# Another written order of all engines and queues, and a tile of its own for the products of dots and softmax weights, in a one-core kernel with a hand-written issue order

## The chip, the cores and the metric

The kernel runs on one core of one Trainium2 chip. The metric is the device time of one execution in microseconds; a time is the median of several runs. Five engines work side by side, each through its own list of instructions in the order in which the program wrote them: TensorE (PE, with its weight loads PEld), VectorE (DVE), ScalarE (ACT), GpSimd (POOL, which here issues the gathers and the accumulating stores) and SyncE (SP, which issues all other transfers). Transfers run on 16 DMA engines. An engine waits at the head of its list when an input is not there; what stands behind waits with it.

## What is computed

An input `x` of 2048 rows by 448 columns is normalised, and three things are added: `x` itself, a state-space convolution (S4) and a layer of 4096 tiny experts (PEER, 16 heads, one expert for each head and row).

```python
    def _A_ref(u, A_re, A_im, B_re, B_im, C_re, C_im, log_dt, Dskip):
        ...
        P = jnp.exp(logdA[:, :, None] * l[None, None, :])
        K = jnp.einsum("dn,dnl,dn->dl", Cc, P, dB).real
        ...
        y = (lambda x, *d: x.transpose(*d))(y, 0, 2, 1) + u * Dskip[None, None, :]
        return y

    def _B_ref(x, w_q, k1, k2, u, v):
        ...
        s1 = jnp.einsum("nhd,ed->nhe", q1, k1)
        s2 = jnp.einsum("nhd,ed->nhe", q2, k2)
        i1 = jnp.argsort(-s1, axis=-1)[..., :K]
        i2 = jnp.argsort(-s2, axis=-1)[..., :K]
        ...
        g = _softmax(top_s, axis=-1)
        ue = u[top_e]
        ve = v[top_e]
        act = _gelu(jnp.einsum("nd,nhkd->nhk", xf, ue))
        out = jnp.einsum("nhk,nhk,nhkd->nd", g, act, ve)
        return out.reshape(B, S, D)

    x = A_u
    xn = _layernorm(x, axis=-1)
    return x + _A_ref(xn, A_A_re, ...) + _B_ref(xn, B_w_q, B_k1, B_k2, B_u, B_v)
```

The elided part of `_A_ref` convolves every column with its kernel `K` by FFT.

## The kernel before

The work is cut into some 3,400 small steps. A step belongs to one engine, and steps of one kind form a stream (`e_d`, `s4_v`, ...), in which they keep their sequence. `plan()` makes the streams; `Plan.run` then walks a constant string, `ORDER`. Each character names a stream, and the next step of that stream is written. So `ORDER` alone fixes the sequence on every engine and every queue. Buffers come from rings: a step takes a slot and a later step gives it back. The largest ring has 22 slots of 128 x 1024 floats; gathered rows (`ue`), layer-norm tiles, combined weights, products of the convolution and transfers to and from DRAM all share it, and a new tile gets the slot that has been free longest. Waits between engines follow from which tiles a step reads and writes, not from the list of dependencies in the plan, which only forbids orders.

The streams that the text speaks of, with their lines:

- Scores: the weights are combined with the keys on PE (`w_p`, L862), a layer-norm tile is transposed (`sc_t`, L943), scores are made on PE (`sc_p`, L961 and L970), and DVE and ACT find the best key (L985 to L1048). The indices go to DRAM and come back (`ix_st`, `ix_ld`).
- Experts, 16 tiles of rows with 4 groups each, 64 groups: four gathers on POOL (`e_g`, L1083) bring 896 floats for each row, the expert's u and v side by side. DVE makes the dot product of each (`e_d`, L1091). Then, on 128 x 4 numbers, a tanh form of gelu: ACT squares the dots (L1098), DVE makes the cubic (`e_v1`, L1101), DVE multiplies the dots by the softmax weights (`e_v1`, L1110), ACT takes the tanh (L1104), DVE joins the two (`e_v2`, L1107) and spreads the result over a mask (`e_v2`, L1114), and PE uses that as weights to add up the v halves (`e_p`, L1121). After the last group of a tile, ACT copies the sum out (`o_a`, L1132) and POOL adds it to the output in DRAM (`o_st`, L1135).
- S4, 56 batches of 8 columns: exponentials and angles, sines on ACT (L629 to L635), four products on DVE (`s4_v`, L660 to L666), a product on PE (`s4_k1`, L682), a copy on ACT (`s4_k2`, L690), a small addition on DVE (`s4_k2b`, L693), PE again (`s4_k3`, L702), a copy on ACT (`s4_k4`, L706).
- Convolution, in four chunks of columns; the last chunk has 64 of them: PE (`cu1`, `cv1`; L762, L779 for the last chunk), DVE products (`cv3`, L808, in the last chunk L786), PE (`cv5`, L830, last L825), ACT (`cv6`, L837), a store to `t_d` (`cv7`, L842). Then the tiles are loaded back (L1165), multiplied on PE (L1177), and added to the output: for three chunks over ACT and POOL (`f_p`, `f_a` L1184, `f_st` L1191), for the last chunk on DVE (`g_v`, L1181), which reads the output back first (`g_b`, L1155) and stores it (`g_st`, L1189).

The order is written in time: the string starts with loads and layer norm, mixes scores, S4 and experts through the middle, and ends with the last chunk.

Of the kernel before, what the change touches and what calls it, by code (L numbers as in the profile page):

```python
# [172 lines left out]
ORDER = (
    "41H444446H4447H244024HHHH424HH6H4H2H7H12H4HHHHHII7H42H1HNCC42H7282O42D2E842HH8748HH121CDH4CD2KHF4HEE1D14E224HFL4H4CKL7DC"
    "I472K24F72EC4I4F3MD7777E7Y3C5QFJLKL9D56DCEFEP47F48D47C9F9EM8KQLQ48D9FwK97774E7FC4L8K44DCJA947E449YC87C9JFDD47E46H7RF4798"
    "AL8QRCEARF7ADCZDEDRFEFEFKQRHwQLNORHGQ9RHQQPH9SaRRMRTQZHTRQYQNATRRHTRHHJOATSTQQTTTTBRTeHReTTGQTUVQGHbYVMHHWRRQQHHXHxxcHee"
    "RRRPdfSNgxgOyfeHgHHwgQwQIHHIyxPfQKyHgygzggxRQJ!gRT!gHhRYTQLTGRzHgQhTKh#xgHRLxTfRMRNOPeSQygyJxXgx#TQ$yTxgeHQHTfQTyTThxTzR"
    "!HgRg!bHxTfgxRgzTQRe#Q#yyyUycgdz$NybxxRO!Qch!ezRyVQHhH#Rdebyi#STTVIIgxRRHThhYwj$gwyzh!QxK!wgyHQzWTLHRwRQKxLRQHRxy#TN#kR$"
    "HxPMhShghyxyxHOHizxaygHQXH!TyxTjTeK!QThJLTyy%kbXeRzhHRQ&RQKRiJzxP#jHf!Qg#$!eyHHLYRQzhggHkfRghieHHRxxgxSf#jK#ykTyI$lLKTgg"
    "LMeTyZlzmTKm!x!LlKyxzmLlN#xUHM#Tyx$IOgggTxgQTYQwKPhHHQyHfHQyTRwgzLwg!R!gQxhgRhRKgzMhyHTe#HfJHgHw#gLmQxHeehxx$yRyhiNRReeO"  # L180
    "yxjkfgzQQ!gVHVhSP!xg%yTyHzJxTyTHx#QRT#gHxTTyQglRHzThchQ$gH!hTIMdKgg!YQR&TIxRRLWmyYKLiNJhjhzfyR#OgUJk#R$ihaQHjexPyVyHxHeH"
    "zKSkMxgegy!x!hHQfTLHRKzyTexLgMR#g#eVQhfH$HbRgQgwQwglhyWxwZTxXygghyHwHzlRggRmHmH!Yg!TRzyTxiQf#xjke#RHy$HSNOHHIyhxTxlTz!TT"
    "TXXK!yTghQLTzQ#yeTPegxhKhgJhx%#fgmeyxgyIQxyezyLifg$Hjg!cQbRkRhKTg!YgLRzxlKh#UQHg#MgVgx$dQygaRLxHiNyhHxHmzOfPQeygw!R!xjhy"
    "ggzkefgyRRSgxyQ&##RHwQRThhzRVw!HHH$fxTQl!zH##QRehHQgRgiyRHHxgeWRSxewNMHjHxO$HhkTIyhgQgZKLyTxQhlJyTxmyTgKLRigmTQzhx!T!zIx"
    "#xygyMfJ%xgJXTQyPeRRTRg#hx$TgTjfzekQKgy!TRgx!Lxfyhz#y#lTegQRxKUgc$LmeNRSVxVeayOhWhzywQ!hTQiQyRjxgy!hQzygwhRPhXzgxgMT#Rxk"
    "g#ih$R!xdg!xgQQexfwzxy#ZwTRjRhTgkRT#yyNOx$hQxSeTx%ylegfx&zey!gQTyTxgfPT!RTzyyTTexQQgTlgz!#T!#z#myR$yhQQ#UyRVgyRxRxxywz!N"
    "OgiRRy$xP!jSzmhyQhX#yklwn#hgxTxQ$RmTRgwwgVQgixxhhnxhgeefz!yyyy!ggWfxzehjkTxQQx##gTgeXfzyRgl$TQyRRxm!eg!yRzR&%#xhx-Sn#xyz"
    "y!yyn$ioTpT!gzhTaoy#gbqzxojo!h#pqxpcqnyTghgxT!onypzyoTwdgTTp#k$ghigqT#refexhyeXxhqwz!hgxyehsgof!&zUxpoxsepwjXg$wgqpykf#q"
    "nogpghhxoyVbxq#gypqiggg$hnxrg%izxoxyhyjxgyg!kf!Vqyzx&ez##sgghp$ex!xqsooxyfp!zxpjyZ#ge#yk$eetgoqhfggWhqhrggxsynozyhghygoh"
    "sxlxwm!xtwpy!lticgywxpqmdaz#wzi!jgk!l#qghexpXqXhzbejkf#hy$#xhhyghegxmlfhyxe$gylyxge%mxzf!hgmrslg!yzm#igjk#gxnghhlgm$hyix"  # L190
    "gs&jyxyzZkhygghf!xlmg!z#exyyhijz#exhge!fkeggyy!tyfgeggzlghgc(gy$hhw#(ihxjwxdmhg)#zka!*gxhg$x!hifezjkelg#xwglm+f#xege$xxh"
    "wxgfgxy%yhgyyegy)gzi*yg!jh!ghkyzhmlxgfg(xh#gmxZ#g$iyx(hej)hhykhg*feezegigyjxy!fk!+zegg+#alxgmyg#lzy!!wbgzhyh#yfmg)xgxg$h"
    "*hexgyhghigfze#gjgxfgywhk$wx!hlix!+gyZemeecgx-xXwz#gghjyydzgklm#!yhfgghy!e$zgoo#%poggheq#yyohppfegqix$ohpzgyxq!yx!pqhxfg"
    "yyz#xnjeox&xpgrqzgqs#cyo!!oephiqgpoagkqzh$#dfwxgsngogphgrp#gxgyhyfqyqoxZx$ygjewhhgystipkhzfxeox!oq!zghjgohee#swpqrwkeyig"
    "g#hhygpsgojbxtyqhypxsxzp!ogyk!fgz$lhmhqxitpgxqeqhjy#&begkzeegrhles!fxsml#gxm%xytxhlmxy&nl!zm#giyfxjyZkggg#zgygwah!h$glh("
    "mhfgx!ygheeghygz#igj$hexfkyhe(lgzegf#gwgxmg!!x$)gwgyiyygzhxhcxg*xd##hwjykz!n+$glmh!ixhfg(ezgyeyh)%j#xkxeeghfg#yxg(f*gyh)"
    "eyygg$c*zlghimgZh!jggdxkyh!zla)bgmyhfghx#*i+ggfh#gxgeh&x$ehxxzj+yfekgyge!ie!xyggzjgkyghxgzfhx#hlh!mg#gwl$whmei+hh!ggfxxg"
    "ezhgfwyjgwey-gex#yg#xeiyzgxyg!kal$yj!zx%yxhyxghmkz#hc!#hg$ydglxeghfyymggixfgheyegfe!jzh#k#xezg!ylg!Zxgzxhggyy#iggh$yhz#$"
    "wwg!jhkmlymxfwoheyxexh!giphgwqego&oypfxepqqyz#ohx#yxggoz!ppfqg!yjy$gxzeoyr#gqxxozphngigqkoxpgs#%aq!yxo!z$yhpg#ghqejsfpno"
    "gehyrggphs&hyxe#tzfgq$kegofgnxygi!qg!jhexzphxouxqpo#gvnk#ghyqywwpxgwhg$qsihgojyfyezg!kx!pzqopehetgrghhsshoyny#whfuglxlx#"  # L200
    "qmpgymiefvjhgzx$egxgykulx!gmlg!x%yqytxnihymzglgghxhxghr&shhhzixjs#j#k!lvh$mmy!kizxt##jlkyl(ymum$vooqoqyzqy!x!rs)yq,qsqry"
    "(*zsosrsq#xy(zsq)!+!r)*sts+t#t$t*(z#.#+$%.)/:&.-//.::/*;+;;:;")


class Kernel:
# [861 lines left out]
    def experts(s, t):  # L1067
        p = s.p
# [8 lines left out]
        for g in range(4):  # L1077
            Q = {}
            u = (4 * t + g) / 64
            for c in range(4):  # L1080
                def ga(c=c, g=g, Q=Q):
                    ue = Q["ue", c] = s.flat("q", "ue", 2 * D)
                    s.nc.gpsimd.indirect_dma_start(  # L1083
                        out=ue, out_offset=None, in_=s.io["uv"],
                        in_offset=bass.IndirectOffsetOnAxis(ap=s.IDX[t][:, c, g:g + 1].bitcast(U32), axis=0))

                def do(c=c, Q=Q):
                    if c == 0:
                        for k in ("dot", "x2", "th"):
# [1 line left out]
                    s.nc.vector.scalar_tensor_tensor(Q["ue", c][:, :D], Q["ue", c][:, :D], 1.0, B["xr", c], op0=ALU.mult, op1=ALU.mult,  # L1091
                                                     accum_out=Q["dot"][:, c:c + 1])
# [4 lines left out]
            def a1(Q=Q):
                s.nc.scalar.activation(Q["x2"], Q["dot"], AF.Square)  # L1098

            def v1(Q=Q):  # L1100
                s.nc.vector.scalar_tensor_tensor(Q["x2"], Q["x2"], 1 / 0.044715, Q["dot"], op0=ALU.add, op1=ALU.mult)  # L1101

            def a2(Q=Q):
                s.nc.scalar.activation(Q["th"], Q["x2"], AF.Tanh, scale=math.sqrt(2 / math.pi) * 0.044715)  # L1104

            def v2(Q=Q):
                s.nc.vector.scalar_tensor_tensor(Q["th"], Q["th"], 1.0, Q["dot"], op0=ALU.add, op1=ALU.mult)  # L1107

            def v2b(g=g, Q=Q):
                s.nc.vector.tensor_tensor(out=Q["dot"], in0=Q["dot"], in1=s.IDX[t][:, :, 4 + g].bitcast(F32), op=ALU.mult)  # L1110

            def v2c(Q=Q):
                Q["A"] = s.sm.tile([128, 4, 32], F32, name="A", bufs=2)
                s.nc.vector.tensor_tensor(out=Q["A"], in0=s.mask[:, None, :].to_broadcast([128, 4, 32]),  # L1114
                                          in1=Q["th"][:, :, None].to_broadcast([128, 4, 32]), op=ALU.mult)

            def m2(g=g, Q=Q):
                if g == 0:
                    B["po"] = s.pst([128, 512], "po", "po")
                for c in range(4):  # L1120
                    s.nc.tensor.matmul(B["po"][32 * c:32 * c + 32, :D], Q["A"][:, c], Q["ue", c][:, D:],  # L1121
                                       start=(g == 0), stop=(g == 3))
# [138 lines left out]
```

## Time and profile before

| what | value |
|---|---|
| median of 3 runs | 810.61 us (805.64 to 812.17) |
| the profiled execution | 807.42 us, of which its span is 805.7 us |
| busy share of the span | PE 82%, DVE 85%, ACT 66%, POOL 44% |
| mean granted TensorE clock | 0.906 |

A row of the profile's groups gives the source line, the engine, the operation and its tiles, how often it ran, its busy time and the mean of one in nanoseconds, then the time that the engine stood idle just before it and what ended most of that. A row of the waits gives who waited for whom, the total, the number of times and the longest. A row of the timeline gives the start and the duration, and in brackets the idle time before. A row of the stretches gives, for each engine, busy time and number of instructions, then the granted clock, the busy share of the DMA engines and what they moved.

### The profile page before, as it was taken

What the parts mean: (1) busy time and instruction counts of PE and PEld (TensorE: products, weight loads), DVE (VectorE), ACT (ScalarE), POOL (GpSimd) and SP (SyncE); (2) the same over time, 40 slices, a digit from 0 to 9 for tenths busy, and PEclk for the clock granted to TensorE, in tenths of its full rate; (3) what the DMA queues carried; (4) which work ended last, traced back from release to release, by engine and by line L of the source; (5) the groups of instructions that cost most, each with busy time, mean ns of one, the idle gap of its engine ahead of it and who ended that gap; (6) DMA issues with size and microseconds to landing.
All of it is one profiled execution on the core that took longest, in us unless ns stands there. A gap on an engine that the chain in (4) does not pass through costs nothing.

```text
span 805.7 us, 19880 instructions
## 1 busy us (share of the span) xinstructions
PE 664.6 (82%) x7628; PEld 361.1 (45%) x7628; DVE 686.9 (85%) x1727; ACT 533.3 (66%) x1069; POOL 351.6 (44%) x303
## 2 busy tenths in 40 slices
...
PEclk9999999999999999999999995678997665699896
...
GB/s 313 348 335 263 259 224 175 232 204 249 275 199 242 202 202 255 180 252 270 366 300 312 304 286 286 292 291 276 206 286 344 319 222 269 252 264 287 271 253 175
DMA packets 139975, 212.36 MB, mean 264 GB/s; under 512 B 45096, under 2 KB 121896, under 8 KB 139816
## 3 DMA queue, kind: packets, MB, share of 16 engines
q0 software_dynamic: 29120, 124.27, 49.9%
q1 hardware_dynamic: 110760, 86.81, 35.5%
...
## 4 chain that ended last, share of the span: by engine, by line
DVE 33%; PE 24%; ACT 15%; DMA 15%; issue 9%; POOL 2%; SPq 1%; POOLq 0%; DVEq 0%; ACTq 0%
PE sc L961 8%; DVE ue L1091 7%; DMA ue<-in_uv_dram,ig 6%; DVE ph L614 4%; PE wc L862 3%; DVE mg L666 3%; PE po L1121 3%; DVE zi L662 2%; DVE cp L808 2%; ACT CS L635 2%; DVE mx L985 2%; ACT CS L629 2%; ACT CS L632 2%; PE sc L970 2%; PE up L724 2%
## 5 line engine op out<-in xcount | busy, mean ns | idle before, releaser
L1083 POOL DMA_INDIRECT ue<-in_uv_dram,ig x256 | 308.2, 1204 | 364.2 <-PE po L1121 101.4
L961 PE MATMUL sc<-W,xt 128*128 128x512 f32 x384 | 181.2, 611 | 8.6 <-ACT xt L946 7.8
L1091 DVE SCALAR_TENSOR_TENSOR ue<-ue,xr 128x448 f32<-128x448 f32 x256 | 155.7, 619 | 26.0 <-DMA ue<-in_uv_dram,ig 24.1
L961 PEld LDWEIGHTS sc<-W,xt 128*128 128x128 f32 x384 | 69.3, 191 | 100.8 <-issue 86.2
L1121 PE MATMUL po<-ue,A 128*32 128x448 f32 x512 | 74.0, 654 | 23.4 <-DVE A L1114 9.2
L682 PE MATMUL kp<-mg 128*32 128x64 f32 x1792 | 65.8, 244 | 22.2 <-DVE mg L666 7.9
L590 ACT ACTIVATE mg<-lg 128x512 f32<-128x512 f32 x112 | 63.1, 603 | 17.2 <-PE lg L579 16.7
L682 PEld LDWEIGHTS kp<-mg 128*32 128x32 f32 x1792 | 48.1, 124 | 49.4 <-issue 13.2
L662 DVE TENSOR_TENSOR zi<-mg,CS 128x1024 f32<-128x1024 f32 x56 | 68.3, 1219 | 0.0
L666 DVE TENSOR_TENSOR mg<-mg,CS 128x1024 f32<-128x1024 f32 x56 | 68.3, 1219 | 0.0
L682 PE MATMUL kp<-zi 128*32 128x64 f32 x1792 | 65.7, 242 | 0.0
L614 DVE CUSTOM_DVE_ANT_0 ph<-st,ph 128x512 uint16<-128x512 uint16 (+2 forms) x84 | 65.2, 776 | 0.5
L635 ACT ACTIVATE CS<-CS,halfpi 128x1024 f32<-128x1024 f32 x56 | 64.4, 1150 | 0.8
L629 ACT ACTIVATE CS<-ph 128x1024 f32<-128x1024 int32 x56 | 62.0, 1107 | 3.9 <-DVE ph L614 3.1
L632 ACT ACTIVATE CS<-ph 128x1024 f32<-128x1024 int32 x56 | 62.6, 1117 | 0.0
L702 PE MATMUL vp<-f,kt 128*64 128x128 f32 x448 | 41.3, 317 | 19.5 <-DVE kt L693 11.3
L985 DVE TENSOR_REDUCE mx<-sc 128x8 f32<-128x512 f32 x64 | 43.7, 683 | 14.5 <-PE sc L970 9.6
L682 PEld LDWEIGHTS kp<-zi 128*32 128x32 f32 x1792 | 50.3, 126 | 0.2
L579 PE MATMUL lg<-lc,rt 32*128 32x512 f32 x112 | 38.8, 544 | 12.0 <-ACT mg L590 7.9
L830 PE MATMUL ip<-cp,e 64*128 64x256 f32 x384 | 44.7, 382 | 2.9 <-DVE cp L808 2.8
L702 PEld LDWEIGHTS vp<-f,kt 128*64 128x64 f32 x448 | 27.5, 155 | 43.1 <-DVE kt L693 16.7
L798 PE MATMUL U<-VU,g 128*64 128x128 f32 x384 | 41.3, 294 | 6.0 <-ACT us L803 3.4
(244 smaller groups left out, 1219.2 us busy)
## 6 DMA issues: line engine op xcount, KB each, us to landing
...
ue<-in_uv_dram,ig POOLq DMA_INDIRECT x256
...
```

The costliest lines, as they stand in the source:

```text
L614: s.nc.vector.tensor_tensor(out=rw(n, 2 * n), in0=rw(0, n), in1=o["st"][:, k, b0:b0 + 2].rearrange("p b h m x -> p (b h m x)")[:, None].to ...
L629: s.nc.scalar.activation(CS[:, 1].rearrange("p (m r x) -> p m r x", r=16, x=2), four(s.ph), AF.Sin, scale=SC)
L632: s.nc.scalar.activation(B["CS"][:, 0].rearrange("p (m r x) -> p m r x", r=16, x=2), four(s.ph), AF.Abs)
L635: s.nc.scalar.activation(B["CS"][:, 0], B["CS"][:, 0], AF.Sin, scale=-SC, bias=s.halfpi)
L662: V.tensor_tensor(out=zi[:, 512:], in0=mg[:, 512:], in1=CS[:, 1], op=ALU.mult)
L666: V.tensor_tensor(out=mg[:, 512:], in0=mg[:, 512:], in1=CS[:, 0], op=ALU.mult)
L682: s.nc.tensor.matmul(kp[32 * c:32 * c + 32, 64 * gi:64 * gi + 64], T[ri][:, 1024 + m:1056 + m], view(T[ri], m, [[512, 2], [1, 32]]), start ...
L702: s.nc.tensor.matmul(vp[64 * ri:64 * ri + 64, 128 * gi:128 * gi + 128], B["kt"][:, 64 * gi:64 * gi + 64], s.f1[:, ri], start=True, stop=True)
L961: s.nc.tensor.matmul(B["sc", q].rearrange("p a b -> p (a b)"), B["xt"][:, i], w, start=(q % 2 == 0 and i == 0), stop=(q % 2 == 1 and i == 2))
L1083: s.nc.gpsimd.indirect_dma_start(out=ue, out_offset=None, in_=s.io["uv"], in_offset=bass.IndirectOffsetOnAxis(ap=s.IDX[t][:, c, g:g + 1].b ...
L1091: s.nc.vector.scalar_tensor_tensor(Q["ue", c][:, :D], Q["ue", c][:, :D], 1.0, B["xr", c], op0=ALU.mult, op1=ALU.mult, accum_out=Q["dot"][: ...
L1121: s.nc.tensor.matmul(B["po"][32 * c:32 * c + 32, :D], Q["A"][:, c], Q["ue", c][:, D:], start=(g == 0), stop=(g == 3))
```

## The change

`ORDER` is another string of the same length, with the same number of characters for every stream; every engine and the SP queue get another sequence. Of 538 steps on PE 122 keep their place and a step moves by 1.9 places on average; on DVE 87 of 1429 keep it (6.5 places on average, at most 90), on ACT 115 of 863 (3.2), on SP 47 of 285 (3.6). The 256 gathers keep their places among each other, and of the 28 accumulating stores on POOL 25 keep theirs among each other.

In `experts`, the product of the dots and the softmax weights (L1110) goes to a tile `dw` of its own in place of overwriting `dot`, and the plan lets it follow the dots directly; its stream still puts it behind the cubic of the same group. The join (L1107) reads `dw`.

```diff
 ORDER = (
-    "41H444446H4447H244024HHHH424HH6H4H2H7H12H4HHHHHII7H42H1HNCC42H7282O42D2E842HH8748HH121CDH4CD2KHF4HEE1D14E224HFL4H4CKL7DC"
...
-    "qmpgymiefvjhgzx$egxgykulx!gmlg!x%yqytxnihymzglgghxhxghr&shhhzixjs#j#k!lvh$mmy!kizxt##jlkyl(ymum$vooqoqyzqy!x!rs)yq,qsqry"
-    "(*zsosrsq#xy(zsq)!+!r)*sts+t#t$t*(z#.#+$%.)/:&.-//.::/*;+;;:;")
+    "44H444HH1HH2704HH7HH2HHH46HH7HH24444I6H4444H47H8CH22NI2H4241DE4HHC88142OC78D4D127H4H1EKECH74C44FLKF4CHHDL47HDEEFKDFFL24H"
...
+    "%gkuolhgmileqxhpwlgjyxzhtmxiqhg!!gjmggzrxglshshklkhuh#hlmmmhhyytij&x#kxixxyyjvz!$xv(kxllmymo!oqqqryysqszox(rs#y#yy)o$ysz"
+    "y!zz!#!tz!*#q,q()#q#rtss($qr*+)ts$+s*t..+).//%&::-./:/*;;:+;;")
...
-                        for k in ("dot", "x2", "th"):
+                        for k in ("dot", "x2", "th", "dw"):
                             Q[k] = s.sm.tile([128, 4], F32, name=k, bufs=2)
...
             def v2(Q=Q):
-                s.nc.vector.scalar_tensor_tensor(Q["th"], Q["th"], 1.0, Q["dot"], op0=ALU.add, op1=ALU.mult)
+                s.nc.vector.scalar_tensor_tensor(Q["th"], Q["th"], 1.0, Q["dw"], op0=ALU.add, op1=ALU.mult)
 
             def v2b(g=g, Q=Q):
-                s.nc.vector.tensor_tensor(out=Q["dot"], in0=Q["dot"], in1=s.IDX[t][:, :, 4 + g].bitcast(F32), op=ALU.mult)
+                s.nc.vector.tensor_tensor(out=Q["dw"], in0=Q["dot"], in1=s.IDX[t][:, :, 4 + g].bitcast(F32), op=ALU.mult)
...
             y = p.add("e_a", "ACT", 100, a1, deps=[v])
-            y = p.chain("e_v1", "DVE", [(75, v1), (75, v2b)], deps=[y])
+            y = p.add("e_v1", "DVE", 75, v1, deps=[y])
+            yw = p.add("e_v1", "DVE", 75, v2b, deps=[v])
             y = p.add("e_a", "ACT", 100, a2, deps=[y], tset="E|S|A")
-            y = p.chain("e_v2", "DVE", [(75, v2), (dv(128), v2c)], deps=[y, s.C["mask"]], take=("A",), give=("gel",))
+            y = p.chain("e_v2", "DVE", [(75, v2), (dv(128), v2c)], deps=[y, yw, s.C["mask"]], take=("A",), give=("gel",))
```

In the string, `x` is a gather, `y` a dot, `z` an ACT step of the gelu, `!` is `e_v1`, `#` is `e_v2`, `$` is `e_p`; `h` is `s4_v`, `i` `s4_k1`, `j` `s4_k2`, `k` `s4_k2b`, `l` `s4_k3`, `m` `s4_k4`; `u` is `cu1`, `o` `cv1`, `q` `cv3`, `r` `cv5`, `s` `cv6`, `t` `cv7`; `%` is `o_a`, `&` `o_st`; `(`, `)`, `*`, `+` are the load, PE, ACT and POOL steps of the first three chunks' ends, and `-`, `.`, `/`, `:`, `;` those of the last chunk (read back, load, PE, DVE, store).

More of the change, by code (lines that the diff above doesn't have):

```diff
@@ L178 @@
[L178 to L197, printed above, removed]
@@ L198 @@
-    "ezhgfwyjgwey-gex#yg#xeiyzgxyg!kal$yj!zx%yxhyxghmkz#hc!#hg$ydglxeghfyymggixfgheyegfe!jzh#k#xezg!ylg!Zxgzxhggyy#iggh$yhz#$"
-    "wwg!jhkmlymxfwoheyxexh!giphgwqego&oypfxepqqyz#ohx#yxggoz!ppfqg!yjy$gxzeoyr#gqxxozphngigqkoxpgs#%aq!yxo!z$yhpg#ghqejsfpno"
-    "gehyrggphs&hyxe#tzfgq$kegofgnxygi!qg!jhexzphxouxqpo#gvnk#ghyqywwpxgwhg$qsihgojyfyezg!kx!pzqopehetgrghhsshoyny#whfuglxlx#"
-    "qmpgymiefvjhgzx$egxgykulx!gmlg!x%yqytxnihymzglgghxhxghr&shhhzixjs#j#k!lvh$mmy!kizxt##jlkyl(ymum$vooqoqyzqy!x!rs)yq,qsqry"
@@ L202 @@
-    "(*zsosrsq#xy(zsq)!+!r)*sts+t#t$t*(z#.#+$%.)/:&.-//.::/*;+;;:;")
+    "44H444HH1HH2704HH7HH2HHH46HH7HH24444I6H4444H47H8CH22NI2H4241DE4HHC88142OC78D4D127H4H1EKECH74C44FLKF4CHHDL47HDEEFKDFFL24H"
+    "27EC4J42HMF2HDC227KLI272223QEI47DC44E4346CDFFDK441C4QE4C9FDE978L88FDRQ9M4CREE94J74497J75RCKF5F8LQ4KCD977R71D4wE77E9778CL"
+    "FFDEDAE6YFF7AYK9QHHLQANH7OQRHR9GR8S8AH9wQZH9HRaTwRHAQGHeRQYTHRQTHGQTRTRYHNHRHOSTQJTAQGMTHTeTHbQTRTTReTQUcQdQRVeNfRIVOWgg"
+    "PXRQRfQPPPxBRRggHSxQTfgRxTyHeTRggIRZxTgwMXJxQKTyxHLyyfgQKLgzxQRh!!HRNRyyOz#xSPyyHQgzT!MH#QQxxggzgJTT$h!RyhTxRxR#HQRgfhgT"
@@ new lines @@
+    "#HQyTbghyh$yzQx!fHz!#NxyReOyiQ#TeHTHx$gyxRwYHeyxRTwxzQeUKHSeVQR!whgLhHwRjgHgcQQKQx!PRydzgY#yHRLHTbyIJRINHR#ThgThHx$bhHhH"
+    "TOgKcLkRHVaTyMSdxgzxgT!!QiHxQzRyKHxQj#eHTyPTQRTyTHhxQfyTz!Hk#H%LggRRz$JhQMxH!iHjRRfhHRgxKg#TLHkyIfYhygTW#exyeTSexiX$KLYg"
+    "lxKlLNMeyjzO!IHQzHgxKy!mygLPK#yTkTMxmQ#Hyl$ggwJQRHhzLRh!Thgmg!HezQfxhRex#gK#eQHwRwxThheHyxLgRgHR$y%QfggRHNxxOUiyjwfyzQ!z"
+    "TMx!hy#byZSQggVVT#cQeHxyHRykHlgHHgzx$a!hRxJHgQ!gQHzTIYmhKTy&x#gLTh#digXIKTeQRyRTLJYP$fNjggTRhRlxOgeHyyHkHQzfKgh!gLxmzHHh"
@@ new lines @@
+    "T!yexxlHPiH#QmjeRHTK#SJWHhRHhf$yxQgLgURXeggRhQyhHkYgyVgQiz!gQzg!TlMHwTHeHVNMRgHw#HRTIj#xbww&xmxxhOkh$eTyeQPRRhSxyKhTQlfT"
+    "eyyLIgJe%zy!T!QxRXmzQxYT#xKT#T$gLfyHyxKRTgQLgfyhzHHRx!!RhxzMg#QNxg#Hh$ggOyyiTHhxjKTTyHyggzUHR!RkHhPxcR!hZiQQQyRxgazSd#Qf"
+    "jyHxygkRgLH#RlHRgyzhh$iHMw!TeHT!HVQHhRmgfQNHgz#eO#$Rgx%xwIfThyRTjKTWygSQxwxekVLeJTKlQlywyexQxggLPxzIQ!gygR!TTyRRmgzhgxRi"
+    "TT#Q#gyy$QjzhZ!zexx!gkhMTKxefLhgTXKe#Thh#yyTRJh$imReLegfxNggOyRyfxMyhggxyQQz!!xxUgzxRyS#gjWagh#RlQ$QQRkyTThRglQwXzThgmgg"
```

18 lines of the change are left out of this document (15 added, 3 removed).

## The prediction

> **What bounds the kernel now.** I read the page first: the busy shares, the DMA queues and the chain that ended last.
>
> ```profile
> span 805.7 us, 19880 instructions
> PE 664.6 (82%) x7628; PEld 361.1 (45%) x7628; DVE 686.9 (85%) x1727; ACT 533.3 (66%) x1069; POOL 351.6 (44%) x303
> PEclk9999999999999999999999995678997665699896
> q0 software_dynamic: 29120, 124.27, 49.9%
> q1 hardware_dynamic: 110760, 86.81, 35.5%
> DVE 33%; PE 24%; ACT 15%; DMA 15%; issue 9%; POOL 2%; SPq 1%; POOLq 0%; DVEq 0%; ACTq 0%
> ```
>
> Three resources are near their limit together: DVE at 85%, PE at 82%, and the DMA engines at 49.9 + 35.5 = 85.4% of the span. None of them owns the chain (DVE has a third of it). A new sequence of the same work can take only idle time; DVE has 805.7 - 686.9 = 118.8 us of it. The second view, busy time by stage, says where.
>
> ```profile
> 0.00:150.00 150.00, 124.81 (x444) 51.11 (x445) 111.70 (x240) 72.04 (x169) 28.12 (x35) 1.00 0.80 272
> 150.00:400.00 250.00, 230.39 (x1839) 99.16 (x1838) 232.35 (x628) 158.44 (x341) 111.31 (x97) 0.99 0.77 240
> 400.00:750.00 350.00, 272.50 (x4579) 182.87 (x4577) 319.57 (x800) 285.50 (x520) 196.83 (x158) 0.82 0.94 282
> 750.00:806.00 56.00, 36.91 (x768) 27.95 (x768) 23.29 (x63) 17.28 (x40) 15.30 (x15) 0.80 0.94 230
> ```
>
> The columns after the stretch are PE, PEld, DVE, ACT, POOL, the clock and the DMA share. DVE's idle time is 38.3 us up to 150 (PE is the bound there once the weights come in), 17.7 us from 150 to 400 (PE and DVE both at 92 to 93%), 30.4 us from 400 to 750 (DVE 91%, DMA 94%), and 32.7 us in the last 56. The third view is DVE's waits, first from 100 to 760, then from 760 to the end.
>
> ```profile
> DVE ue L1091 <- DMA ue<-in_uv_dram,ig: 24.1, 23, 2.9
> DVE kt L693 <- ACT kt L690: 6.1, 7, 1.8
> DVE th L1107 <- ACT th L1104: 3.3, 7, 1.6
> ...
> DVE bb L1181 <- PE po L1177: 13.5, 4, 11.1
> DVE cp L786 <- PE U L779: 4.3, 2, 2.6
> DVE th L1107 <- ACT th L1104: 3.6, 1, 3.6
> DVE kt L693 <- ACT kt L690: 2.6, 1, 2.6
> ```
>
> In the middle, dots that wait for their gather are the largest item, 24.1 us in 23 waits; in the tail the waits are a chain of steps that cannot overlap. These two places carry the forecast.
>
> **The change part by part.** *The tile `dw`.*
>
> ```profile
> L1110 DVE TENSOR_TENSOR dot<-dot,ig 128x4 f32<-128x4 f32 x64 | 10.2, 160 | 0.4
> 763.03 0.20 ACT L1104 ACTIVATE th<-x 128x4 f32<-128x4 f32 x1
> 763.11 0.16 DVE L1110 TENSOR_TENSOR dot<-dot,ig 128x4 f32<-128x4 f32 x1
> ```
>
> The 64 products keep their 160 ns. Before, too, the tanh did not wait for the product: it starts at 763.03, the product of the same group at 763.11. Only the plan's list tied them, and in the stream the product still follows the cubic, which has waited for the square already. So the tile by itself is worth 0; its cover is that no wait existed. Bounds: 0 to the 0.4 us that DVE idled before L1110. No instruction is added or removed, and the changes of function set on ACT, each a table load, number 61 in both strings.
>
> *The start.*
>
> ```profile
> 18.12 1.33 PE xtp L943 x5
> 103.36 1.58 DMA idx_d<-ix
> ```
>
> PE now begins with the combined weights and not with the transposes that waited for the first layer norm. Only the 1.33 us of transposes can be gained, if the weights are there sooner; but from PE step 38 to 58 the sequence is the same as before, so I take 0. Against it: the index store that starts at 103.36, on which all gathers hang, now has 3.3 us more DVE work written ahead of it (layer-norm steps, two angle steps, two maxima of the next tile). The first dots also stand behind 3.3 us more work, which covers it; price 0, bounds -1.3 to +3.3. On SP the weight loads move ahead of a layer-norm load and an `xr` load; on its own list the last of them is at place 58, before at 62. Covered while PE is busy; without the cover it is within these bounds.
>
> *The middle.* Thousands of moves can't be priced one by one, so I count distances in the two strings, with each step's duration from the trace.
>
> ```profile
> L1083 POOL DMA_INDIRECT ue<-in_uv_dram,ig x256 | 308.2, 1204 | 364.2 <-PE po L1121 101.4 <-issue 47.0 <-DMA ig<-idx_d 46.6
> L1091 DVE SCALAR_TENSOR_TENSOR ue<-ue,xr 128x448 f32<-128x448 f32 x256 | 155.7, 619 | 26.0 <-DMA ue<-in_uv_dram,ig 24.1 <-DMA xr<-xn_d 0.9 <-PE vp L702 0.8
> ```
>
> Gathers wait mostly for a slot that PE must free (101.4 us). Counting takes and gives of the 22-slot ring, 4.3 slots are free on average when a gather is written before, 5.2 after; for gathers 64 to 95 it is 3.0 against 5.6. With 430 takes in some 760 us, 0.9 of a slot means a release 1.6 us earlier. Against it, the DVE work written between a gather and its dot falls from 6.2 to 5.6 us on average. The net, 1.0 us earlier, stands beside a mean wait of 24.1/23 = 1.05 us. Were it uniform, nearly all 24.1 us would go; it is not (the distance to the dot rises for some gathers and falls for others), and from 400 on the DMA engines are 94% busy. I take a quarter, -6, with the ends -24 and +23 (the second is a rival below). For the small addition L693, 21 of 56 have under 1 us of DVE work between ACT's copy and themselves before, 10 after: half of the 6.1 us goes, -3, ends -6 and 0. The sines' products (17 against 16 of 448 under 1 us) and the joins behind the tanh (17 against 14 of 64 under 0.3 us) hardly change: 0. That is -9 of DVE waiting. Where DVE stops waiting, PE or the DMA engines are late next, at 92% and 94% in the stages; I count 0.6 of it, between the chain's third and all: -5.4, say -5.
>
> *The tail.* Here the sequence can be followed step by step.
>
> ```profile
> 752.10 0.63 DVE L1091 SCALAR_TENSOR_TENSOR ue<-ue,xr 128x448 f32<-128x448 f32 x1 [1.77 <-DMA ue<-in_uv_dram,ig]
> 761.43 1.22 DVE L666 TENSOR_TENSOR mg<-mg,CS 128x1024 f32<-128x1024 f32 x1
> 762.64 1.72 PE L1121 MATMUL po<-ue,A 128*32 128x448 f32 x8
> 768.25 0.96 PE L1121 MATMUL po<-ue,A 128*32 128x448 f32 x8
> 769.14 3.02 PE L779 MATMUL U<-VK,g 128*64 128x64 f32 x96
> 770.34 1.29 DVE L786 TENSOR_TENSOR cp<-us,U 128x512 f32<-128x512 f32 x2 [2.65 <-PE U L779]
> 779.37 0.68 DVE L786 TENSOR_TENSOR cp<-us,U 128x512 f32<-128x512 f32 x1
> 780.97 2.00 PE L825 MATMUL ip<-cp,e 64*128 64x256 f32 x16
> 785.31 0.96 PE L1121 MATMUL po<-ue,A 128*32 128x448 f32 x8 [0.45 <-DVE A L1114]
> 787.25 0.86 POOL L1135 DMA_DIRECT2D out_dram<-ob  x1 [1.05 <-ACT ob L1132]
> 787.25 6.86 DMA out_dram<-ob
> 794.91 3.88 DMA tl<-t_d
> ```
>
> Let V be the end of the last S4 product, 762.65 before. (a) In the new order four dots, numbers 244 to 247, stand behind V and not before it: 4 x 0.62 = 2.5 us, and one of them waited 1.77 us for its gather. V comes up to 4.3 us earlier; ACT's sines may stop it sooner, so I take 3.4. (b) Before, PE ran the sum of group 60 (1.72 us) between V and the last batch's product, and that of group 61 (0.96 us) ahead of the last chunk's products, which start at 769.14, V + 6.5. Now the first follows the last batch's product and the second the chunk's first products. The small addition (L693) stands behind the four dots, at about V + 3, and with some 1.5 us through L702 and L706, an estimate, L779 starts at V + 4.5. (c) From there DVE has more to do than before, seven dots and some ten small steps besides the eight products: 8 x 0.68 + 7 x 0.62 + 2 = 11.8 us against the 9.7 from 770.34 to 780.05. It starts 1.2 us after L779, as before, so the last product ends at V + 17.5, as it did (780.05 is V + 17.4). (d) Before, the last expert sum (785.31, V + 22.7) waited for the tanh, 3.6 us late in ACT's list; now the tanh comes first, and the sum follows the last L825 and one L1177 of about 1.1 us, at V + 20.6: 2 us earlier. The accumulating store at 787.25 (6.86 us to land) and the load behind it (3.88 us) close the run and shift with it. Together -5.4. Against it, the last gather now waits for the first L779 group and its dot stands ahead of the last four products; a late one holds the convolution, 0 to 2 us. POOL's list keeps the last stores behind the last gather. I take -4, ends -7 and +2.
>
> [...]
>
> ```profile
> 758.76 0.19 PEld L682 LDWEIGHTS kp<-mg 128*32 128x32 f32 x8 [3.71 <-ACT tq L837]
> 760.00:765.00 5.00, 3.40 (x49) 2.00 (x53) 3.77 (x13) 1.46 (x5) 0.38 (x1) 0.50 0.66 209
> 604.74 1.10 PE kp L682 x64
> 685.92 1.86 PE kp L682 x64
> ```
>
> After the gap of 3.71 us the clock is 0.50, and a batch of L682 takes 1.10 us in one place and 1.86 in another. [...]
>
> *The sum.* -4 - 5 = -9 against the profiled execution's 807.42 gives 798.4. The median, 810.61, stands 3.2 us above that execution, so I forecast 798.4 + 3.1 = 801.5 for a median.
>
> **The rivals.** *No net gain.* With PE, DVE and the DMA engines within 3% of each other, a wait shortened on one shows again on the next; for it speaks the chain without an owner. The middle gives 0 and the tail up to -4: 806.6 to 810.6.
>
> *Slower, through gathers that come too late.* 30 of 256 gathers have under 1.5 us of DVE work between them and their dot, before 22. If the eight each paid the longest wait seen, 2.9 us, that is +23, of which 0.6 counts, +14; less the tail's 4, +10: 810.6 + 10 = 820.6. It decides once the dots wait over 20 us more than their 24.1. The DMA share of 0.94 speaks for it, the older slots against.
>
> [...]
>
> *The change does nothing.* The tile alone does nothing; the order as a whole can't be said to do nothing, so this falls into the first rival.
>
> **How the numbers follow.** A measurement of this kernel tells about 1% from no change, 802.5 to 818.7. The forecast has 0.48, of which 0.37 lies under 802.5 and 0.11 above. No net gain has 0.30 (0.03 faster, 0.22 within, 0.05 slower, since the unpriced moves go both ways). Late gathers have 0.15 (0.02 within, 0.13 slower). The clock has 0.07 (0.05 and, with wider gaps, 0.02 slower). Together faster 0.45, same 0.35, slower 0.20. The far ends of the middle, (-24 - 6) x 0.6 = -18, and of the tail, -7, give 785.5 together; under 1 in 10 lies so far, and I cut at 788. Above, 1 in 10 is left over 819, most of it the slower rival's upper half. The forecast's own range is 793 to 807.
>
> **What would show it.** Right: dots waiting for gathers fall from 24.1 to near 18 us and L693 for ACT from 6.1 to near 3 in the middle; the first L779 comes within 5 us of the last L666; the last L1114 no longer ends a wait of the last L1121, and the end follows V by about 41 us and not 43. Wrong: gathers' waits over 40 us; a dot in the last 30 us that waits for its gather and holds L786; or DVE waits gone with the span unchanged, and PE or DMA rows grown in their place.

## The result, and the profile after

| | before | after |
|---|---|---|
| median | 811.39 us (805.64 to 813.06) | 778.76 us (776.25 to 781.38) |
| ratio | | 0.961, 95% interval 0.956 to 0.966 |
| the profiled execution | 807.42 us | 777.9 us |

The change makes the kernel 32.6 us faster by the medians, 29.5 us by the two profiled executions. The forecast was 801.5 us with a range of 788 to 819: the direction was right, but the gain is more than three times the 9 us that were forecast, and the time lies below the range. Some kernels below ran in groups of runs in which the kernel before itself took 857 to 862 us and not 811 (the last section), so each is compared through its ratio to the kernel before beside it; the changed kernel itself was never run in such a group.

The page of the changed kernel. Lines behind L1121 carry a number one higher than before.

```profile
span 776.1 us, 19859 instructions
PE 658.5 (85%) x7628; PEld 358.9 (46%) x7628; DVE 680.7 (88%) x1727; ACT 535.7 (69%) x1071; POOL 351.3 (45%) x303
PEclk9999999999999999999899997566996767699995
q0 software_dynamic: 29120, 124.27, 50.2%
q1 hardware_dynamic: 110760, 86.81, 36.8%
DVE 30%; PE 29%; DMA 19%; ACT 12%; issue 7%; POOL 1%; SPq 1%; DVEq 0%; ACTq 0%; POOLq 0%
L1083 POOL DMA_INDIRECT ue<-in_uv_dram,ig x256 | 307.3, 1200 | 334.4 <-PE po L1121 87.1
L1091 DVE SCALAR_TENSOR_TENSOR ue<-ue,xr 128x448 f32<-128x448 f32 x256 | 155.8, 619 | 17.4 <-DMA ue<-in_uv_dram,ig 11.6
L1121 PE MATMUL po<-ue,A 128*32 128x448 f32 x512 | 70.1, 616 | 10.2 <-issue 3.9
```

The work is the same, packed closer: every busy share rises, DVE's to 88%, and still nobody owns the chain. The granted clock is 0.908 on average against 0.906, so the clock is not the reason.

Where did the 29.5 us come from? The stretches of the changed kernel are cut here so that DVE has done about the same work at each border as at 150, 400 and 750 us before (columns: PE, PEld, DVE, ACT, POOL, clock, DMA share, GB/s).

```profile
0.00:146.00 146.00, 124.61 (x510) 51.52 (x514) 110.92 (x239) 69.94 (x164) 30.97 (x37) 1.00 0.83 281
146.00:387.00 241.00, 226.87 (x1772) 97.58 (x1766) 229.43 (x628) 163.66 (x348) 111.68 (x94) 0.99 0.78 246
387.00:722.00 335.00, 271.70 (x4574) 182.98 (x4574) 317.28 (x798) 286.28 (x523) 194.29 (x162) 0.83 0.96 300
722.00:777.00 55.00, 35.28 (x776) 26.83 (x776) 23.09 (x65) 15.80 (x38) 14.38 (x12) 0.80 0.90 213
```

Read against the prediction's rows, the four stages give 4, 9, 15 and 1.5 us (the last row of each table reaches past the end of its span). In the two middle ones DVE idles 241 - 229.4 = 11.6 and 335 - 317.3 = 17.7 us, before 17.7 and 30.4: 18.8 us of the 24. The other 5.2 us are its busy time. What is left of its waits, from 100 to 730 us:

```profile
DVE ue L1091 <- DMA ue<-in_uv_dram,ig: 10.8, 12, 2.4
DVE mx L985 <- PE sc L970: 7.1, 3, 4.9
DVE ue L1091 <- DMA xr<-xn_d: 5.6, 4, 3.6
DVE x L1101 <- ACT x L1098: 3.2, 6, 1.2
DVE mx L985 <- PE sc L961: 1.8, 3, 1.4
DVE kt L693 <- ACT kt L690: 1.6, 3, 0.6
DVE zi L660 <- ACT CS L629: 1.6, 3, 0.6
...
DVE th L1107 <- ACT th L1104: 0.5, 2, 0.3
```

The dots' waits for gathers went from 24.1 to 10.8 us, the small addition's from 6.1 to 1.6. The joins fell from 3.3 to 0.5. Other items grew (scores, rows of `xr`, the cubic), by less than what went.

Idle time is not all of it. In the traces, the durations of all of DVE's instructions add up to 807.8 us in both kernels, but the time in which at least one runs (the busy time of the page) falls from 686.9 to 680.7 us: an instruction that follows another directly starts some 80 ns before the other has ended. Before, DVE stood still 233 times, after 148 times. 85 stops fewer at 80 ns are 6.8 us, about the 6.2 us by which the busy time shrank. By these two traces a stop cost that overlap besides its own length.

The tail, as a timeline (start, duration; in brackets the idle time before and what ended it). V, the end of the last S4 product, is 729.85:

```profile
728.64 1.21 DVE L666 TENSOR_TENSOR mg<-mg,CS 128x1024 f32<-128x1024 f32 x1
734.09 2.09 PE L779 MATMUL U<-VK,g 128*64 128x64 f32 x64 [0.47 <-ACT VK L706]
747.03 0.68 DVE L786 TENSOR_TENSOR cp<-us,U 128x512 f32<-128x512 f32 x1
751.05 0.96 PE L1121 MATMUL po<-ue,A 128*32 128x448 f32 x8
766.71 0.42 DVE L1182 TENSOR_TENSOR bb<-po,bb 128x256 f32<-128x256 f32 x1 [19.00 <-PE po L1178]
```

The convolution starts at V + 4.2 and its last product ends at V + 17.9. The end comes at V + 46.2. From the chain that ended last, two transfers:

```profile
753.06 8.74 DMA t_d<-tq
763.17 6.13 DMA tl<-t_d
```

Here the loads of the last chunk's tiles stand behind a store to `t_d` that takes 8.74 us, and the load that closes the run takes 6.13 us. Before, this chain ran over the store of the last sum (6.86 us) and a load of 3.88 us.

### The profile page after: what moved, and what is told of

Read it like the earlier page. It is cut to its first block, busy times and chain, and to the rows that moved or that the text cites. A ratio compares the mean times of both kernels' runs of the same rounds, so it can differ in the third digit from the quotient of the medians.

```text
span 776.1 us, 19859 instructions
## 1 busy us (share of the span) xinstructions
PE 658.5 (85%) x7628; PEld 358.9 (46%) x7628; DVE 680.7 (88%) x1727; ACT 535.7 (69%) x1071; POOL 351.3 (45%) x303
## 4 chain that ended last, share of the span: by engine, by line
DVE 30%; PE 29%; DMA 19%; ACT 12%; issue 7%; POOL 1%; SPq 1%; DVEq 0%; ACTq 0%; POOLq 0%
PE sc L961 10%; DMA ue<-in_uv_dram,ig 7%; DVE ue L1091 7%; DVE zi L662 3%; DVE ph L614 3%; DVE mg L666 3%; DMA xr<-xn_d 3%; PE wc L862 3%; PE kp L682 2%; PE sc L970 2%; ACT CS L629 2%; PE ip L830 2%; ACT CS L632 2%; DVE cp L808 2%; PE up L724 2%
## 5 line engine op out<-in xcount | busy, mean ns | idle before, releaser
L1091 DVE SCALAR_TENSOR_TENSOR ue<-ue,xr 128x448 f32<-128x448 f32 x256 | 155.8, 619 | 17.4 <-DMA ue<-in_uv_dram,ig 11.6
L1121 PE MATMUL po<-ue,A 128*32 128x448 f32 x512 | 70.1, 616 | 10.2 <-issue 3.9
L682 PE MATMUL kp<-mg 128*32 128x64 f32 x1792 | 64.1, 240 | 14.9 <-DVE mg L666 6.5
L590 ACT ACTIVATE mg<-lg 128x512 f32<-128x512 f32 x112 | 63.2, 597 | 18.7 <-PE lg L579 17.9
L682 PE MATMUL kp<-zi 128*32 128x64 f32 x1792 | 63.4, 238 | 0.0
L682 PEld LDWEIGHTS kp<-mg 128*32 128x32 f32 x1792 | 46.5, 121 | 35.3 <-issue 8.6
L985 DVE TENSOR_REDUCE mx<-sc 128x8 f32<-128x512 f32 x64 | 43.7, 683 | 14.5 <-PE sc L970 10.8
L579 PE MATMUL lg<-lc,rt 32*128 32x512 f32 x112 | 40.4, 564 | 14.4 <-ACT mg L590 10.8
L682 PEld LDWEIGHTS kp<-zi 128*32 128x32 f32 x1792 | 48.8, 123 | 0.1
L798 PE MATMUL U<-VU,g 128*64 128x128 f32 x384 | 42.2, 299 | 5.4 <-DVE cp L808 3.4
```

The lines of the kernel that those rows point to most:

```text
L682: s.nc.tensor.matmul(kp[32 * c:32 * c + 32, 64 * gi:64 * gi + 64], T[ri][:, 1024 + m:1056 + m], view(T[ri], m, [[512, 2], [1, 32]]), start ...
```

## The experiments

"Old" and "new order" are the strings before and after. A string spliced from both keeps each stream in sequence. Where a diff below writes the string as a formula (`new[0:1600]` and the like), the formula stands for the string itself.

**The tile.** Two kernels separate the two parts of the change.

```diff
-                        for k in ("dot", "x2", "th", "dw"):
+                        for k in ("dot", "x2", "th"):
...
-                s.nc.vector.tensor_tensor(out=Q["dw"], in0=Q["dot"], in1=s.IDX[t][:, :, 4 + g].bitcast(F32), op=ALU.mult)
+                s.nc.vector.tensor_tensor(out=Q["dot"], in0=Q["dot"], in1=s.IDX[t][:, :, 4 + g].bitcast(F32), op=ALU.mult)
```

> The new order with the product of dots and weights written over the dots again, as before (no tile dw). Theory A (the gain is all in the order; the tanh never waited for the product): within 1% of the changed kernel, 775 to 783 us, ratio to the kernel before 0.955 to 0.966. Rival B (the tile of its own carries a part of the gain, through joins and next-group dots that no longer wait): at least 8 us of the 32.6 us come back, 787 us or more.

Measured: 779.7 us, ratio 0.960 (0.954 to 0.966). The other half, the changed kernel with the old string:

```diff
 ORDER = (
-    "44H444HH1HH2704HH7HH2HHH46HH7HH24444I6H4444H47H8CH22NI2H4241DE4HHC88142OC78D4D127H4H1EKECH74C44FLKF4CHHDL47HDEEFKDFFL24H"
+    "41H444446H4447H244024HHHH424HH6H4H2H7H12H4HHHHHII7H42H1HNCC42H7282O42D2E842HH8748HH121CDH4CD2KHF4HEE1D14E224HFL4H4CKL7DC"
...
```

> The old order with the tile dw. Theory A (order alone): no change against the kernel before, ratio 0.995 to 1.005, about 811 us. Rival B (tile): at least 8 us faster, 803 us or less.

Measured: 812.9 us, ratio 0.999 (0.995 to 1.004). The tile alone does nothing that these intervals show, and the order alone gives the whole gain. Theory A holds, B falls.

**Halves.** The strings were joined at step 1600: first new then old, and first old then new.

```diff
 ORDER = (
-    new[0:3421]
+    new[0:1600] + [what is left, in the sequence of old]
```

> Tile dw; the first 1600 of the 3421 written steps as in the new order, the rest in the old order's sequence. Theory C (the gain builds up evenly over the run, because many small waits go everywhere): at step 1600 the changed kernel is 15 us ahead (386 against 371 us), which stays, so 811 - 15 = 796 us, and the other half of the gain is lost. Rival D (one place in the second half carries it, the lead at step 1600 is lent, and the work it saved shows up again as waits later): 805 us or more. Rival E (all in the first half): 785 us or less.

Measured: 804.9 us, ratio 0.991 (0.987 to 0.994).

> Tile dw; the first 1600 written steps in the old order, the rest in the new order's sequence. Theory C (even build-up): the 18 us that the changed kernel wins behind step 1600 remain, 811 - 18 = 793 us. Rival D (one place in the second half): 785 us or less. Rival E (all in the first half): 805 us or more. If neither half holds its share (both kernels at 805 or more), the two halves work only together.

Measured: 794.8 us, ratio 0.980 (0.973 to 0.986). Together the halves give 7 + 17 = 24 of the 32 us. The second half comes within 2 us of C, the first lies at the border of D, so none of C, D and E is met cleanly. In the trace of the first half, its lead is there at the border (14.5 us at the S4 product 64), but eight products later 5 us are left: the seam, the place where the two orders join, takes most of it. DVE's waits in that kernel from 355 to 410 us:

```profile
DVE eq L992 <- DMA xn_d<-xx: 7.0, 1, 7.0
```

DVE waits 7 us for one slot of the ring, which a store of a layer-norm tile still reads. Neither order has this wait there; it comes from joining them.

**The tail.** The same at step 3190, some 69 us before the end, first the new tail on the old order.

```diff
 ORDER = (
-    old[0:3421]
+    old[0:3190] + [what is left, in the sequence of new]
```

> The old order up to written step 3190 (of 3421, about 737 us), then the new order's sequence. The prediction's term for the tail was -4 us (ends -7 and +2). From the two traces, the changed kernel gains 3.9 us between the S4 product 208 and the end of the run (its lead grows from 25.6 to 29.5 us). So 4 us faster than the kernel before, ratio 0.990 to 0.998. Rival (the tail's gain hangs on what stands before it): ratio 0.999 or more.

Measured: 808.4 us beside 813.6, ratio 0.988 (0.982 to 0.995). Its counterpart (`new[0:3190]`, then the sequence of old) and the changed kernel again:

> The new order up to written step 3190 (about 709 us), then the old order's sequence. By the tail's term: 4 us slower than the changed kernel, so its ratio to the kernel before is 0.005 higher than that of the changed kernel in this call. Rival: the old tail is as good behind the new middle, or better, since in the trace the end follows the last S4 product by 46 us in the changed kernel and by 43 us in the one before: up to 3 us faster than the changed kernel.

> The changed kernel again, beside the kernel before on whatever clock this chip grants now. In the call with the moved dots the kernel before took 862 us, not 811, with the granted clock at 0.93 from 150 to 400 us where the first trace has 0.97 to 1.00. If the kernel before is at about 811 here: ratio 0.955 to 0.966, as first seen. If it is at about 860: theory F/G (the gain is DVE's waits) says that PE is then the bound and part of the gain goes, ratio 0.97 to 0.99; rival K (the new order saves PE's time too, by shorter gaps) says 0.96 or less there too.

Measured: 782.8 us (0.964; 0.959 to 0.969) and 777.2 us (0.956; 0.951 to 0.961). So the new tail on the old order is worth 5 us by the medians and 10 by the ratio, whose interval reaches down to the 4 us forecast; the profiled execution shows 3 us. Behind the new order it is worth 6 us, but the two intervals overlap, and the profiled execution with the old tail took no longer than that of the changed kernel (776.8 and 777.1 us). In its second profile the changed kernel ends 42.2 us behind V, and the new order with the old tail ends 42.3 us behind it. In the kernel before it is 43.0. So 46.2 belongs to one execution, and single traces do not tell the 2 us between the two tails.

**Waits taken out by hand.** If DVE's waits have a price each, the old order must gain when the steps that wait are written later. In the old string 22 dots moved, and 17 other steps that hang on them followed (here a `y` goes some characters to the right):

```diff
-    "HxPMhShghyxyxHOHizxaygHQXH!TyxTjTeK!QThJLTyy%kbXeRzhHRQ&RQKRiJzxP#jHf!Qg#$!eyHHLYRQzhggHkfRghieHHRxxgxSf#jK#ykTyI$lLKTgg"
+    "HxPMhShghyxyxHOHizxagHQXH!TyyxTjTeK!QThJLTyy%kbXeRzhHRQ&RQKRiJzxP#jHf!Qg#$!eyHHLYRQzhggHkfRghieHHRxxgxSf#jK#ykTyI$lLKTgg"
```

> Old order (tile dw), in which only the 22 dots that waited on DVE for their row before 740 us (23.4 us of waits in the trace of before) are written later, each behind as much other DVE work as it waited, plus 0.4 us; 17 other steps that hang on them follow. Theory F (each of DVE's waits counts nearly in full, wherever it stands, and the gathers' are the most of it): 15 us or more faster, 797 us or less. Theory G (the factor of 0.6 of the prediction): 23.4 x 0.6 = 14 less what comes back as new waits, 798 to 803 us. Rival H (a wait removed shows again on PE or on the DMA engines, the gain came from elsewhere): 806 us or more.

Measured: 868.4 us beside 862.0, ratio 1.009 (1.003 to 1.015). As the kernel before took 862 us there, the same kernel was run again:

> The old order with the 22 late dots moved behind other DVE work, again (it was 1.009 of the kernel before where that took 862 us). If the kernel before is at about 811 here, the three accounts stand as before: F (waits count in full) 797 us or less; G (0.6) 798 to 803 us; H (what is removed comes back as other waits) 806 us or more. If it is at about 860 again: 1.00 to 1.01 again.

Measured: 814.5 us beside 813.6, ratio 0.998 (0.994 to 1.002): no gain, rival H. DVE's waits from 100 to 740 us show why, first of the kernel before:

```profile
DVE ue L1091 <- DMA ue<-in_uv_dram,ig: 21.7, 21, 2.9
...
DVE zi L660 <- ACT CS L629: 4.6, 6, 1.9
...
DVE mx L985 <- PE sc L970: 1.3, 1, 1.3
...
DVE x L1101 <- ACT x L1098: 0.9, 4, 0.3
```

and of the one with the moved dots (second run):

```profile
DVE mx L985 <- PE sc L970: 10.5, 4, 6.3
DVE zi L660 <- ACT CS L629: 10.1, 7, 4.9
DVE kt L693 <- ACT kt L690: 7.3, 10, 1.8
DVE th L1107 <- ACT th L1104: 6.8, 7, 1.7
DVE x L1101 <- ACT x L1098: 6.6, 13, 1.8
DVE ue L1091 <- DMA ue<-in_uv_dram,ig: 6.6, 11, 1.1
```

The dots' waits fall by 15.1 us, as meant. The scores' rise by 9.2, the waits of the sines' products by 5.5, the cubic's by 5.7, the joins' (3.3 before) by 3.5 us. Part of this differs between traces of the same order anyway: in the kernel with the first half new, whose order behind the seam is the old one, the cubic waits 3.0 us and the joins 6.5 us from 410 to 805 us, in the kernel before 1.0 and 5.9; for the sines' products it is 2.1 against 2.5. The reading that fits is that what stood behind a dot now comes sooner, before its own input is there, and what hangs on the dot comes later. DVE's idle time as a whole did not fall (740 - 644.3 = 95.7 us in the first 740, against 740 - 653.6 = 86.4), and over the whole run DVE's waits that the profile lists come to 116.4 us in 98 waits, before to 107.8 us in 90. The small steps were moved in the same way, here two joins (`#`) behind two dots (`y`):

```diff
-    "!HgRg!bHxTfgxRgzTQRe#Q#yyyUycgdz$NybxxRO!Qch!ezRyVQHhH#Rdebyi#STTVIIgxRRHThhYwj$gwyzh!QxK!wgyHQzWTLHRwRQKxLRQHRxy#TN#kR$"
+    "!HgRg!bHxTfgxRgzTQReQyy##yUycgdz$NybxxRO!Qch!ezRyVQHhH#Rdebyi#STTVIIgxRRHThhYwj$gwyzh!QxK!wgyHQzWTLHRwRQKxLRQHRxy#TN#kR$"
```

> Old order (tile dw), in which only 13 small steps of DVE that waited for ACT before 740 us (the addition behind ACT's copy, the cubic and the join behind square and tanh; 11.1 us of waits) are written later, each behind as much other DVE work as it waited, plus 0.4 us. Theory F (full): 10 us faster, 801 us. Theory G (0.6): 7 us, 805 us. Rival H (comes back elsewhere): within 2 us of before, 810 us or more.

Measured: 863.6 us beside 862.0, ratio 0.995 (0.989 to 1.002): not told from none. The interval also holds the 7 us of theory G (0.991).

**One group of streams at its new places.** Every step gets its place in the old string as its rank, the steps of one group (experts, then S4) their place in the new one.

```diff
 ORDER = (
-    old, by rank in old
+    old, by rank in old; steps of the group by rank in new
```

> Old order, in which the experts' steps (gathers, loads of rows, dots, gelu, sums, stores) stand at the places that they have in the new order, and all others at their old ones (13 steps follow late, for want of a slot). If the gain comes from where the experts stand (their gathers and dots): 790 us or less. If it is spread over experts, S4 and scores: 795 to 803 us. If it needs the S4 steps or the scores to move: 808 us or more.

> The counterpart: old order, in which the S4 steps (with their loads and angles) stand at the places of the new order, all others at their old ones (10 steps follow late). If the gain comes from where S4 stands among the rest: 790 us or less. If it is spread: 795 to 803 us. If the experts' places carry it: 808 us or more.

Measured: 906.9 us, ratio 1.050 (1.031 to 1.069), and 933.6 us, 1.086 (1.073 to 1.099). None of the three accounts foresaw it: either group alone, at the places that it has in the faster kernel, makes the old order much slower. So neither group carries the gain by itself. That it lies in how the groups fit together is argued, not shown: such a splice has seams everywhere, the scores were not moved alone, and both ran beside the kernel before at 862 us only.

**Transfers and slots.** Two resources could still have been the bound: the DMA engines, 96% busy from 387 to 722 us, and the slots of the ring. The narrower gathers read the table as if its rows had 768 floats:

```diff
-                        out=ue, out_offset=None, in_=s.io["uv"],
+                        out=ue[:, :768], out_offset=None, in_=bass.AP(tensor=s.io["uv"].tensor, offset=s.io["uv"].offset, ap=[[768, 4096], [1, 768]]),
...
-                    s.nc.tensor.matmul(B["po"][32 * c:32 * c + 32, :D], Q["A"][:, c], Q["ue", c][:, D:],
+                    s.nc.tensor.matmul(B["po"][32 * c:32 * c + 32, :D], Q["A"][:, c], Q["ue", c][:, 768 - D:768],
```

> The old order with gathers of 768 floats for a row in place of 896 (the table is read as if its rows had 768, and the v part is taken from columns 320 to 767, so the experts' sums are other numbers; instructions on DVE and PE are the same). 16.8 of 212.4 MB go, 10.2 of them behind 400 us. Theory T (behind 400 us the transfers are the bound): 10.2 MB at 300 GB/s, 34 us faster, 770 to 790 us. Theory U (the order's distances between engines are, transfers only through the late dots): at most 10 us faster, 801 us or more.

> The new order with gathers of 768 floats. Theory T: 20 to 34 us faster than the changed kernel, 743 to 758 us (less than the old order if DVE or PE becomes the bound first). Theory U: at most 5 us faster, 772 us or more, since its dots wait only 9 to 12 us for gathers.

Measured: 856.6 us beside 856.9, ratio 1.003 (0.999 to 1.007), and 823.8 us, 0.965 (0.956 to 0.974). 16.8 MB less give nothing to the old order, and the new one comes to about its usual ratio (0.956 to 0.961): theory T falls where it was tried. But from 400 to 750 us that old kernel's DMA share is only

```profile
400.00:750.00 350.00, 263.70 (x3993) 164.46 (x3995) 297.42 (x745) 261.06 (x478) 184.00 (x152) 0.81 0.85 246
```

0.85, where the first trace has 0.94. The two kernels with 21 slots (below), whose gathers are full and which ran beside this one, have 0.86 and 0.88 there: in this group the transfers were less busy even without the narrow gathers. With the kernel before at 811 us, and its share of 0.94, theory T was not tried and stays open.

One slot less:

```diff
-        s.NQ = o["UE"] + o["XX"] + 7 + 3
+        s.NQ = o["UE"] + o["XX"] + 7 + 3 - 1
-        for tag, n in (("xx", o["XX"]), ("W", 7), ("c3", 3), ("eq", 0), ("g", 0), ("vq", 0), ("cA", 0), ("cB", 0), ("tq", 0)):
+        for tag, n in (("xx", o["XX"]), ("W", 7), ("c3", 2), ("eq", 0), ("g", 0), ("vq", 0), ("cA", 0), ("cB", 0), ("tq", 0)):
```

> The new order with 21 slots in the ring in place of 22 (20 steps follow later, where no slot was left). Theory S (free slots at a gather carry the gain: the new order has 0.9 more of them): losing one costs most of the middle's gain, 15 us or more, 792 us or more. If slots matter as in the prediction (6 us of waits for 0.9 of a slot, counted at 0.6): 3 to 6 us slower, 781 to 784 us. If they don't: 780 us or less.

> The old order with 21 slots (31 steps follow later). Theory S: 15 us or more slower, 826 us or more, since fewer slots are free to begin with. As in the prediction: 4 to 8 us slower. If slots don't matter: within 3 us of the kernel before.

Measured: 858.4 us, ratio 1.001 (0.997 to 1.006), and 891.7 us, 1.039 (1.026 to 1.051), beside 856.9. The old order loses 35 us, and the new one, which was not run beside them with 22 slots, falls from its usual 0.956 to 0.961 to the time of the kernel before, as theory S says; but the missing slot also moved 20 steps of the new string and 31 of the old. So the next runs try the opposite, one slot more with the strings nearly untouched:

```diff
-    OPT = dict(UE=8, XX=4, CS=2, ZI=2, MG=4, KT=4, HL=2, SG=1, XR=4, OB=3, XT=1, ST=1)
+    OPT = dict(UE=8, XX=4, CS=2, ZI=2, MG=4, KT=4, HL=1, SG=1, XR=4, OB=2, XT=1, ST=1)
-        s.NQ = o["UE"] + o["XX"] + 7 + 3
+        s.NQ = o["UE"] + o["XX"] + 7 + 3 + 1
-                ig = s.IDX[t - 1 + i] = s.sm.tile([128, 4, 8], I32, name="ig", bufs=16)
+                ig = s.IDX[t - 1 + i] = s.sm.tile([128, 4, 8], I32, name="ig", bufs=7)
```

In the new order `HL` is 1 too, `OB` stays 3, `ttl` has one buffer in place of two, and `ig` has 6.

> The old order with 23 slots in the ring in place of 22: the string is the old one (11 steps of the first weights, of the sums' copies and of the last loads stand some places later, because the room comes from one buffer less of ob, one less of hl, and 7 index tiles in place of 16). A gather then finds on average 5.3 free slots when it is written, as in the new order (5.2), not 4.3. Theory S (free slots carry the middle's gain): ratio to the kernel before 0.970 to 0.985, about 25 us less what the smaller buffers cost. Theory U (the fit of the sequence between engines carries it; one slot less only hurt because of the moved steps): 0.993 to 1.003.

> The new order with 23 slots (8 steps stand later; the room comes from one buffer less of hl, one less of ttl, and 6 index tiles in place of 16). Theory S: the gathers still wait 87 us on POOL for a slot, so a further slot gives something again, less than the first: 5 to 15 us faster than the changed kernel, ratio to the kernel before 0.940 to 0.952, the best of all. Theory U: as the changed kernel, 0.955 to 0.965.

Measured: 855.8 us beside 858.9, ratio 1.000 (0.995 to 1.005), and 833.5 us, 0.975 (0.967 to 0.982). The dots' waits for gathers from 100 to 800 us, first the old order with 21 slots, then with 22 (the kernel with the moved small steps, the nearest trace from such a group of runs), then with 23:

```profile
DVE ue L1091 <- DMA ue<-in_uv_dram,ig: 43.1, 25, 5.2
```

```profile
DVE ue L1091 <- DMA ue<-in_uv_dram,ig: 24.3, 20, 2.9
```

```profile
DVE kt L693 <- ACT kt L690: 24.8, 14, 4.1
...
DVE ue L1091 <- DMA ue<-in_uv_dram,ig: 7.2, 6, 2.7
```

With the extra slot those waits are short, and the old order is not faster for it. So theory S falls where it was tried: more free slots than the string was written for do not carry a gain there. But there the small addition's wait for ACT (L693) is DVE's largest, 24.8 us with 23 slots, where the kernel before at 811 us has 8.7 from 100 to 800 us; in a group with the kernel before at 811 us no other number of slots was tried. The new order is at 0.975 with 23 slots; its ratio with 22 in such a group is not known (0.965 with the narrow gathers), and its buffers are smaller, so this says little. That fewer slots cost so much may be the slot itself or the moved steps; it was not told apart.

## Why the prediction was wrong, step by step

*The tile, 0:* right (0.999 and 0.960). One count was off: ACT's table loads are not equal in number; the trace has 62 before and 64 after.

*The start, 0 with bounds of -1.3 and +3.3:* too little, -4. PE begins with the combined weights at 16.6 us, where it began with transposes at 18.1, and the first score comes to DVE 13.5 us earlier (52.5 against 66.0 us); I had priced only the transposes' own 1.33 us. The 3.3 us against it did not come: the index store starts at 102.61 us, before at 103.36. No run takes the moves of the start apart.

*The middle, -5:* this step failed. The stages between 150 and 750 us gave -24, beyond even the far end of -18. It failed in three places.

1. The list of what changes was too short. Gathers and the small addition were priced; the joins and the sines' products were put at 0 after counting short distances. The joins' waits fell from 3.3 to 0.5 us, the sines' from 4.6 to 1.6, and the 85 stops that no longer happen gave 6 us of overlap that no wait shows, 5.2 of them in these two stages.
2. The size of the gathers' term was derived from free slots (0.9 more, 1.6 us earlier). A whole slot more gives the old order nothing (1.000, beside the kernel before at 859 us), although its dots then wait only 7.2 us. The gathers' term was put at -6; their waits fell by 13.3.
3. The factor. I took a wait on DVE to be worth 0.6 of its length. No factor is right: the moved dots removed 15.1 us and gained nothing, and in the changed kernel the waits that I had priced fell by 13.3 + 4.5 = 17.8 us, not by 9, while those two stages gained 24. With the right falls the factor would still give only 10.7.

What the runs put in place of this: a wait in such a trace is not an item with a price. What counts is DVE's idle time as a whole, with its overlap: it fell by 18.8 us in the two stages, the busy time by 5.2, and that is the 24. (Busy and idle time of an engine always add up to the stage, so this says where the time went, not why.) One kind of wait can go without it (the moved dots). Moving a step gives its distance to the steps behind it, or takes it from them, so it seems that the whole sequence has to improve at once. The new string does that; the two groups of it that were tried alone do not. Which of its moves bring the 24 us, and how much of it hangs on slots or transfers where the kernel before takes 811 us, stays open.

*The tail, -4:* about right in size (5 to 10 us by splices, 3 to 4 by traces behind the S4 product 208, 1.5 by the last stretch), and V + 4.5 and V + 17.5 came out at V + 4.2 and V + 17.9. The last sum came at V + 21.2, not V + 20.6, without the wait for L1114, as foreseen. Wrong was that the last sum's store and the load behind it close the run and shift with it: in the changed kernel's trace other stores and loads of the last chunk close it. The end followed V by 46.2 and 42.2 us in the two traces of the changed kernel, where 41 was forecast.

*The rivals.* No net gain (0.30) and late gathers (0.15) did not come for the change as a whole; for the moved dots alone, no net gain is what came. For late gathers, the counted distances (30 short ones against 22) again said nothing about the waits, which fell. For the clock (0.07), no run shows that gaps on PE set it or what closing them would give; its mean was 0.906 before and 0.908 after.

*The signs to look for.* Gathers and the small addition fell below the values named (10.8 and 1.6 against 18 and 3), which spoke for more than -9 at once.
